# Attention by chunks and a two-layer network: the second layer's C11 seeded in PSUM, three more quarters by seven products, other fillers, and a fixed order

## The chip, the cores and the metric

The kernel runs on one core of one Trainium2 chip. The metric is the time of one execution in device microseconds. Seven names are used for the parts of the core: PE is TensorE (matmuls), PEld its weight loads, DVE VectorE, ACT ScalarE, POOL GpSimd, SP SyncE (it issues DMAs), and PSUM is the memory that TensorE writes, in 8 banks of 2 KB for each of 128 partitions.

## What is computed

```python
# q, k, v: 8 x 8 heads x 576 x 64;  w_in: 512 x 2048;  w_out: 2048 x 512
scores = (q_c @ k_c^T) / 8            # in chunks of 64 tokens
attn   = exp(scores - max) / (sum + 1e-9)
x      = (attn @ v_c)                 # 4608 tokens x 512
h      = x @ w_in
g      = max(0.01 * h, h)
out    = g @ w_out                    # 4608 x 512, float32
```

## The kernel before

**Units of attention.** The 4608 tokens are cut into 36 units of 128 tokens (two chunks, all heads). For a unit u GpSimd issues the loads of q and k (line 93), with a cast to fp16. For the first ten units TensorE transposes q and k (pe_t, lines 404 and 409) against an identity that GpSimd makes; later SyncE does it by DMA (lines 428 and 431). q is put, zero-padded, into QZ (lines 118, 120, 444), and k into KT. The scores go to PSUM (s, tile Sp, line 451). VectorE takes the maximum (m, line 461), subtracts it (b, line 465), ScalarE exponentiates (x, line 471), VectorE sums (z, line 477), adds 1e-9 (ze, line 479), takes the reciprocal (zi, line 481), and VectorE or GpSimd normalises (n, line 487). The result is transposed (e on TensorE, line 495, and its copy d2; or d by DMA, line 506), multiplied with v (v, tile xp, line 517), and ScalarE casts the product into xT (a, line 530), the transposed input of the network, a ring of 1536 tokens. v lies in VB with zeros beside it; for the first batch it is loaded in rows (v_t, line 127) and put in place by copies (v_p).

**Blocks of the network.** The tokens form 12 blocks: 0 to 3 of 128 tokens, 4 to 11 of 512. The plain first layer, mm1(j, a, h), multiplies a column block a of w_in with tokens (tile hT, line 185); for a block of 128 tokens a column block has 512 columns and 16 matmuls. w_in arrives in eight loads, two for each column block of 512 (Q0 to Q3, line 135), w_out in four (P0 to P3, line 141). ScalarE applies the leaky function into gT (line 196). The plain second layer, mm2, serves blocks 0 to 3 (tile oP, line 210).

**Seven products.** For the other blocks matrices are cut in two by two, and the four quarters of a result are made from seven products instead of eight, with sums of the inputs formed ahead: VF and WF of the weights (lines 232 and 235), XF of the tokens (x_form, line 283), S0, S1 and two in-place sums of gT (g_form, lines 342 to 350). Products 1, 6, 7 and 4 pass one after another through a running sum in bank A, products 5 and 3 through bank C, and product 2 uses bank B; C11 is p1 + p2:

```python
B: p2 (with p1: C11)
A: p1, then p6 on top (a copy u2 is taken), p7 (copy u3), p4 (C21)
C: p5 (plus u3 gives C22), p3 on top (plus u2 gives C12)
```

In the first layer (first_fast, tiles hA, hB, hC, line 323) a quarter of a block's columns at a time is treated so; FAST says how many of a block's four quarters, the rest being plain: 4, 3, 4, 2, 4, 4 for blocks 6 to 11, 21 in all. UNIT = 256 cuts blocks 6 and 7 into two halves of 256 tokens each, so that a product there has matmuls of 128 columns in place of 256. In this layer ScalarE seeds bank B with p1 (the step d), and p2 adds to it there. In the second layer (second_fast, tiles oA, oB, oC, line 371), products of blocks 4 to 11 are halved, p = 0 and 1, eight matmuls of 256 columns each. There the step d copies p1 to a temporary, p2 opens its own bank, and VectorE adds the two into the output tile osb (line 235). For the last block (11) the steps work on halves, so that stores can start early.

**What sets the order.** Every step is a Step with its engine, an assumed duration, its inputs, a key, and the PSUM banks and temporaries that it takes and gives. A planner, run(), keeps a clock for each engine and for two DMA queues, picks the step that can begin first (among those within 0.03 us by its key, with hand-set corrections in TUNE), gives out banks and temporaries, and writes the instructions in that order. An engine carries out its instructions in the order written. A table ON names the engine for steps that have a choice. Where TensorE would wait in the first 40 us, the planner puts fillers there, matmuls of 128 columns on the identity (idle, line 535).

Of the kernel before, what the change touches and what calls it, by code (L numbers as in the profile page):

```python
# [16 lines left out]
def kernel(  # L17
# [15 lines left out]
    CH = 64  # L33
# [19 lines left out]
    FAST = {6: 4, 7: 3, 8: 4, 9: 2, 10: 4, 11: 4}  # L53
    UNIT = {6: 256, 7: 256}
    POOL_N, POOL_X, POOL_S = 9, 20, 20
# [139 lines left out]
    def leaky(to, of):  # L195
        nc.scalar.activation(out=to, in_=of, func=AFT.Prelu, bias=0.0, scale=1.0, alpha=0.01)  # L196

    def copy(to, of):
        nc.scalar.activation(out=to, in_=of, func=AFT.Copy, bias=0.0, scale=1.0)  # L199
# [23 lines left out]
    def evict2(j, ti):  # L223
        OSB[j, ti] = osb_tile()[:, 0]
        copy(OSB[j, ti], OP.pop((j, ti)))
# [52 lines left out]
    def x_form(j, h, i):  # L278
# [3 lines left out]
        def less(to, a, b):  # L282
            (nc.gpsimd if j >= POOL_X else nc.vector).tensor_tensor(out=to, in0=a, in1=b, op=ALU.subtract)
# [53 lines left out]
    def g_form(j, i):  # L337
# [5 lines left out]
        if i == 0:  # L343
            plus(SF[j, 0], a21, a22)
        elif i == 1:
            minus(SF[j, 1], SF[j, 0], a11)
        elif i == 2:
            (nc.gpsimd if j >= POOL_S else nc.vector).tensor_tensor(out=a21, in0=a11, in1=a21, op=ALU.subtract)
        else:
            (nc.gpsimd if j >= POOL_S else nc.vector).tensor_tensor(out=a12, in0=a12, in1=SF[j, 1], op=ALU.subtract)  # L350

    def out_product(j, m, p, tag=None):
# [6 lines left out]
        }[m]  # L359
        if j == LAST:  # L360
            key = (j, p, "o" + IN[m])
            if m in OPENS:
                PA[key] = bank([128, HM], "o" + IN[m], tag)
            to, fresh = PA[key], m in OPENS
        else:
            key = (j, "o" + IN[m])
            if m in OPENS and p == 0:
                PA[key] = bank([128, 2, HM], "o" + IN[m], tag)
            to, fresh = PA[key][:, p, :], m in OPENS and p == 0
# [46 lines left out]
    def stage_k(u):  # L416
        KT[u] = sbp.tile([128, 4, 2, CH], FP16, name="KT", tag="KT", bufs=4)
        nc.scalar.activation(out=KT[u], in_=KP.pop(u), func=AFT.Copy, bias=0.0, scale=1.0)
# [50 lines left out]
    def stage_x(u):  # L469
        E[u] = sbp.tile([128, 8, CH], FP16, name="ex", tag="ex", bufs=2)  # L470
        nc.scalar.activation(out=E[u], in_=SH.pop(u), func=AFT.Exp, bias=0.0, scale=SCL)  # L471

    ZI: dict[int, bass.AP] = {}

    def stage_z(u):
        z = sbp.tile([128, 8], FP32, name="z", tag="z", bufs=2)
        nc.vector.tensor_reduce(out=z, in_=E[u], axis=AXL.X, op=ALU.add)  # L477
        ze = sbp.tile([128, 8], FP32, name="ze", tag="ze", bufs=2)
        nc.vector.tensor_scalar_add(out=ze, in0=z, scalar1=1e-9)
        ZI[u] = sbp.tile([128, 8], FP32, name="zi", tag="zi", bufs=2)  # L480
        nc.vector.reciprocal(out=ZI[u], in_=ze)  # L481
# [45 lines left out]
    def stage_a(u):  # L527
        xp = XP.pop(u)
        at = u * G % RING
        nc.scalar.activation(out=xT[:, :, at:at + G], in_=xp, func=AFT.Copy, bias=0.0, scale=1.0)  # L530

    def idle(n, tag):
        t = bank([128, 4, 128], "idle", tag)
        for i in range(n):
            nc.tensor.matmul(out=t[:, i % 4, :], lhsT=ident, rhs=ident, start=True, stop=True)  # L535
# [21 lines left out]
    class Hold:  # L557
# [3 lines left out]
        def fits(self, slots):  # L561
            return [y for y in slots if not self.written or y[1] in written]

    written: set = set()

    class Step:
# [12 lines left out]
    free: dict[str, list[tuple[float, object]]] = {  # L579
        "bank": [(0.0, x) for x in BANKS], "tmp": [(0.0, x) for x in range(NTMP)],  # L580
    }

    class Queues:

        def __init__(self):
            self.now, self.ring, self.out, self.n = 0.0, ([], []), ({}, {}), [0, 0]
            self.done, self.still = 0, []  # L590

        def matmuls(self, n, t):
            self.done += n
            if self.done >= 140:
                self.done -= 128
                if t > STALLS_FROM:
                    self.still.append((t + 0.75, t + 0.75 + STALL))

        def put(self, q, step, at, packets, slow):
            self.ring[q].append([at, packets, slow, step])  # L600
            self.n[q] += 1

        def heads(self):
            return [r[0] if r and r[0][0] <= self.now + 1e-9 else None for r in self.ring]

        def rates(self, h):
            if any(a - 1e-9 <= self.now < b - 1e-9 for a, b in self.still):
                return (0.0, 0.0)
            if h[0] and h[1]:
                return (370.0, 695.0 / h[1][2]) if h[1][2] > 1 else (425.0, 399.0)  # L610
            return (ALONE[0] if h[0] else 0.0, ALONE[1] / h[1][2] if h[1] else 0.0)

        def event(self):
            h = self.heads()
            v = self.rates(h)
            t = [self.now + x[1] / y for x, y in zip(h, v) if x and y]
            t += [r[0][0] for r, x in zip(self.ring, h) if r and not x]
            if any(h):
# [615 lines left out]
```

## Time and profile before

| | |
|---|---|
| time, median of 3 runs | 275.9 us (275.85 to 277.14) |
| profiled execution: span | 273.8 us (from its first to its last instruction; the profile gives no other time of this execution) |
| matmuls / weight loads | 3406 / 3406, of them 86 fillers, all before 18.35 us |
| granted clock of TensorE | 1.00 in every slice |
| DMA | 38.27 MB in 162004 packets; GpSimd's queue carried 18.09 MB, SyncE's 19.41 MB |
| first product of the first layer | 18.35 us |
| end of the last matmul | 270.43 us |

The page of the profile gives busy time by engine, by line and by slice; its views answer for a stretch, a line or a tile. "Idle before" is the time for which an engine stood still ahead of an instruction, and behind it stands what ended the wait. In a view by windows the columns after the stretch and its length are the busy times of PE, PEld, DVE, ACT and POOL with the number of instructions, then the granted clock, the DMA share and GB/s. In a timeline the first two columns are start and length in us. Ends of matmuls are modelled, so a group of matmuls is measured from its start to the next one's start.

### The profile page before, as it was taken

The page shows a single profiled execution, that of the slowest core. Times are in us where ns is not written, and L with a number is a line of the kernel's source. Part 1 is how long each engine was busy: PE and PEld are TensorE (multiplying, and loading weights), DVE is VectorE, ACT ScalarE, POOL GpSimd, SP SyncE. Part 2 cuts the span into 40 slices and gives each one's busy share as a digit, 9 for nine tenths or more (in the row PEclk, how much of TensorE's full clock was granted, in tenths as well). Part 3 has the DMA queues.
Part 4 walks back from the last instruction along what each step waited for, and adds up shares of the span by engine and source line. Part 5 has one row for each costly group of instructions (what it writes and reads, how often), then busy time and mean ns, then how long its engine had stood idle before and what let it go on. Part 6 is the DMA issues. An engine that isn't in the chain of part 4 may idle for free.

```text
span 273.8 us, 8229 instructions
## 1 busy us (share of the span) xinstructions
PE 263.2 (96%) x3406; PEld 238.2 (87%) x3406; DVE 208.2 (76%) x375; ACT 193.9 (71%) x359; POOL 158.9 (58%) x198
## 2 busy tenths in 40 slices
PE   1999999999999999999999999999999999999995
PEld 1889578799999999999999999899999989888884
DVE  5895285789978898899788999897879865831671
ACT  6588947778475644999796369978866896378721
POOL 8999783967898959587758778657351000000000
PEclk9999999999999999999999999999999999999999
DMA  9999999999999999999999999999954100220233
GB/s 134 154 191 183 182 176 176 155 173 217 151 158 152 120 143 208 170 144 234 154 155 121 136 140 247 133 186 197 136 84 151 43 19 2 77 79 0 79 115 116
DMA packets 162004, 38.27 MB, mean 140 GB/s; under 512 B 153008, under 2 KB 157616, under 8 KB 161968
## 3 DMA queue, kind: packets, MB, share of 16 engines
q0 software_dynamic: 114384, 18.09, 97.0%
q1 hardware_dynamic: 46544, 19.41, 42.2%
q8 instruction: 26, 0.43, 0.6%
q10 hardware_dynamic: 1040, 0.26, 0.4%
q14 instruction: 10, 0.08, 0.2%
HBM read 36.70 MB, written 9.44 MB: 169 GB/s over the span
## 4 chain that ended last, share of the span: by engine, by line
PE 90%; ACT 3%; DMA 3%; POOL 2%; issue 1%; DVE 0%; POOLq 0%
PE oA L371 20%; PE hT L185 17%; PE hA L323 14%; PE oC L371 10%; PE hC L323 7%; PE oP L210 5%; PE oB L371 5%; PE hB L323 3%; PE Sp L451 3%; PE xp L517 3%; DMA q_in<-in_q_dram 3%; PE tpe L495 1%; PE idle L535 1%; ACT gT L196 1%; ACT xT L530 1%; PE qp L404 1%
## 5 line engine op out<-in xcount | busy, mean ns | idle before, releaser
L371 PEld LDWEIGHTS <-gT 128*128 128x128 f16 x640 | 61.1, 98 | 6.6
L185 PE MATMUL hT<-xT,w_inT 128*128 128x128 f16 (+1 forms) x864 | 58.6, 225 | 0.1
L185 PEld LDWEIGHTS <-w_inT 128*128 128x128 f16 x864 | 53.1, 98 | 2.0 <-issue 0.4
L444 POOL COPY QZ<-QT 64x512 f16<-64x512 f16 x52 | 36.6, 705 | 20.0 <-DMA QT<-q_in 13.1
L196 ACT ACTIVATE gT<-hT 128x512 f16<-128x512 f32 x60 | 35.1, 599 | 15.9 <-PE hT L185 15.6
L235 DVE TENSOR_TENSOR tmp<-hC,tmp 128x512 f32<-128x512 f32 x42 | 27.9, 678 | 16.6 <-PE hC L323 8.3
L487 POOL TENSOR_TENSOR en<-ex,zi 128x512 f16<-128x512 f16 x22 | 23.8, 1083 | 26.8 <-DVE zi L481 12.3
L323 PEld LDWEIGHTS <-VF 128*128 128x128 f16 x448 | 34.5, 98 | 2.4
L93 POOL DMA_DIRECT2D q_in<-in_q_dram x39 | 33.8, 871 | 4.5 <-DMA w_outT<-in_moe_w_out_dram 1.8
L93 POOL DMA_DIRECT2D k_in<-in_k_dram x39 | 33.5, 863 | 1.2 <-DMA VB<-in_v_dram 0.8
L461 DVE TENSOR_REDUCE mx<-Sp 128x8 f32<-128x512 f32 x36 | 24.6, 684 | 10.3 <-PE Sp L451 10.2
L371 PE MATMUL oA<-WF,gT 128*128 128x256 f16 x256 | 32.2, 273 | 0.0
L199 ACT ACTIVATE tmp<-hA 128x512 f32<-128x512 f32 x42 | 24.3, 602 | 6.8 <-PE hA L323 6.8
L196 ACT ACTIVATE gT<-tmp 128x512 f16<-128x512 f32 x42 | 26.4, 634 | 3.7 <-DVE tmp L235 3.6
L323 PEld LDWEIGHTS <-w_inT 128*128 128x128 f16 x336 | 26.2, 98 | 1.9
L471 ACT ACTIVATE ex<-sh 128x512 f16<-128x512 f32 x36 | 22.8, 633 | 7.0 <-DVE sh L465 6.8
L371 PEld LDWEIGHTS <-S 128*128 128x128 f16 x256 | 24.6, 98 | 2.8
L477 DVE TENSOR_REDUCE z<-ex 128x8 f32<-128x512 f16 x36 | 24.3, 676 | 3.3 <-ACT ex L471 3.2
L530 ACT ACTIVATE xT<-xp 128x512 f16<-128x512 f32 x36 | 21.4, 597 | 7.6 <-PE xp L517 7.4
L465 DVE TENSOR_TENSOR sh<-Sp,mx 128x512 f32<-128x512 f32 x36 | 24.5, 681 | 0.6
L323 PE MATMUL hA<-XF,VF 128*128 128x128 f16 (+1 forms) x224 | 24.7, 246 | 0.0
L199 ACT ACTIVATE tmp<-oA 128x512 f32<-128x512 f32 (+1 forms) x27 | 14.9, 552 | 11.7 <-PE oA L371 11.6
(76 smaller groups left out, 478.7 us busy)
## 6 DMA issues: line engine op xcount, KB each, us to landing
out_dram<-osb SPq DMA_DIRECT2D x14, 512.0 KB, 5.2
VB<-in_v_dram POOLq DMA_DIRECT2D x14, 288.0 KB, 9.1
q_in<-in_q_dram POOLq DMA_DIRECT2D x31, 128.0 KB, 8.3
k_in<-in_k_dram POOLq DMA_DIRECT2D x31, 128.0 KB, 8.4
w_inT<-in_moe_w_in_dram POOLq DMA_DIRECT2D x8, 256.0 KB, 7.5
w_outT<-in_moe_w_out_dram POOLq DMA_DIRECT2D x4, 512.0 KB, 9.0
out_dram<-osb SPq DMA_DIRECT2D x6, 256.0 KB, 5.5
v_t<-in_v_dram POOLq DMA_DIRECT2D x4, 128.0 KB, 7.0
```

Source lines behind the costliest of these rows:

```text
L93: nc.gpsimd.dma_start(out=t[a - u * G:z - u * G], in_=src[b, :, r:r + z - a, :].rearrange("h p d -> p h d"))
L185: nc.tensor.matmul(out=hT[:, i, :], lhsT=w_inT[:, t, fc * 128:(fc + 1) * 128], rhs=xT[:, t, r0 % RING:r0 % RING + tb], start=(i == 0 and t ...
L196: nc.scalar.activation(out=to, in_=of, func=AFT.Prelu, bias=0.0, scale=1.0, alpha=0.01)
L199: nc.scalar.activation(out=to, in_=of, func=AFT.Copy, bias=0.0, scale=1.0)
L235: (nc.vector if e == "dve" else nc.gpsimd).tensor_tensor(out=to, in0=a, in1=b, op=ALU.add)
L323: nc.tensor.matmul(out=PA[key][:, c, :], lhsT=w[:, t, fc * 128:(fc + 1) * 128], rhs=x[:, t, :], start=(m in (1, 5) and c == 0 and t == 0), ...
L371: nc.tensor.matmul(out=to, lhsT=lhs[:, fc, p * 128:(p + 1) * 128], rhs=rhs[:, fc, :], start=(fresh and fc == 0), stop=(fc == HB - 1), skip ...
L444: nc.gpsimd.tensor_copy(out=QZ[u % NQZ][part, :, :, s, :], in_=QT[u][part].rearrange("p i (e t) -> p i e t", e=2))
L461: nc.vector.tensor_reduce(out=MX[u], in_=SP[u], axis=AXL.X, op=ALU.max)
L465: nc.vector.tensor_tensor(out=SH[u], in0=SP.pop(u), in1=MX.pop(u).unsqueeze(2).to_broadcast((128, 8, CH)), op=ALU.subtract)
L477: nc.vector.tensor_reduce(out=z, in_=E[u], axis=AXL.X, op=ALU.add)
L530: nc.scalar.activation(out=xT[:, :, at:at + G], in_=xp, func=AFT.Copy, bias=0.0, scale=1.0)
```

## The change

Six things change.

1. In the second layer the step d copies p1 from bank A into bank B (on ScalarE; in the last block on VectorE), product 2 adds to it there, and a new step c11 copies bank B to osb. VectorE's sum for C11 and the temporary for it go. Product 2 now has the seed among its inputs.
2. FAST is 4 for blocks 7 and 9 too: 24 quarters by seven products instead of 21. No plain quarter is left in blocks 6 to 11.
3. The fillers are matmuls of up to 512 columns on a tile of ones, which VectorE sets with its first instruction (in the memory of XF); the identity isn't needed for them.
4. The three steps of the softmax's denominator become separate (z, ze, zi), and ze may run on ScalarE.
5. More steps have a choice of engine: k, a, copies, seeds, the leaky function (as a two-operand instruction on VectorE), sums for the products (on GpSimd).
6. The planner goes. In its place stand a table ORDER (1478 rows: the number of a step, its fillers, its banks) and a full table ON.

```diff
-    FAST = {6: 4, 7: 3, 8: 4, 9: 2, 10: 4, 11: 4}
+    FAST = {6: 4, 7: 4, 8: 4, 9: 4, 10: 4, 11: 4}
...
+    ones = XF[0][:, 0].rearrange("p t n -> p (t n)")
+    nc.vector.memset(ones, 1.0)
...
-    def leaky(to, of):
-        nc.scalar.activation(out=to, in_=of, func=AFT.Prelu, bias=0.0, scale=1.0, alpha=0.01)
+    def leaky(to, of, e="act"):
+        if e == "act":
+            nc.scalar.activation(out=to, in_=of, func=AFT.Prelu, bias=0.0, scale=1.0, alpha=0.01)
+        else:
+            nc.vector.scalar_tensor_tensor(out=to, in0=of, scalar=0.01, in1=of, op0=ALU.mult, op1=ALU.max)
...
     def idle(n, tag):
-        t = bank([128, 4, 128], "idle", tag)
-        for i in range(n):
-            nc.tensor.matmul(out=t[:, i % 4, :], lhsT=ident, rhs=ident, start=True, stop=True)
+        t = bank([128, 512], "idle", tag)
+        while n:
+            w = min(n, 4) * 128
+            nc.tensor.matmul(out=t[:, :w], lhsT=ones[:, :128], rhs=ones[:, :w], start=True, stop=True)
+            n -= w // 128
...
     def out_product(j, m, p, tag=None):
...
+        opens = m in OPENS and m != 2
...
     def run():
...
+        for i, fill, *slots in ORDER:
+            s = steps[i]
+            if fill:
+                idle(fill[0], BANKS[fill[1]])
+            for h, slot in zip(s.take, slots):
+                h.slot = BANKS[slot] if h.pool == "bank" else slot
             s.emit()
...
+    ORDER = [
+        (57, 0), (6, 0), (56, 0), (8, 0), (66, 0), (60, 0), (55, 0), (1, 0), (63, 0), (65, 0), (58, 0), (0, 0), (62, 0), (2, 0), (53, 0), (13, 0), (52, 0), (61, 0),
...
     def second_fast(j, k0):
...
-        d = cp("d", p1)
-        p2 = mm(2, [g(1, 0) + [p1[1]]] * 2)
+        d = []
+        for p in ps:
+            e, t = on(key + ("d", p), "act", act=us[0], dve=us[1])
+            def seed(p=p, e=e):
+                at = (j, p, "oB") if last else (j, "oB")
+                PA[at] = bank([128, HM] if last else [128, 2, HM], "oB", B1[p].slot)
+                copy(PA[at], psum("oA", p), e)
+            d.append(add(key + ("d", p), e, t, seed, [p1[p]] if last else p1, key=7.0 + k0 / 100, take=[B1[p]]))
+        p2 = mm(2, [[y, p1[1]] + g(1, 0) for y in (d if last else d * 2)])
...
-        s11 = sum_of("d", 0, lo, [x + osb_free() for x in two(p2, d)], B1)
+        s11 = []
+        for p in ps:
+            e, t = on(key + ("c11", p), "act", act=us[0], dve=us[1])
+            s11.append(add(key + ("c11", p), e, t, lambda p=p, e=e: copy(dest(0, lo, p), psum("oB", p), e), ([p2[p]] if last else p2) + osb_free(), key=1.5 + k0 / 100, give=[B1[p]]))
```

Three places show how instructions move. The first is GpSimd's queue at the very start (loads and the identity). The loads of q_in, k_in and v_t are those of units 1 to 3 and of v's first rows; each w_inT row is half of a column block. Before:

```order
L93 DMA q_in<-in_q_dram 128x8x64
L93 DMA k_in<-in_k_dram 128x8x64 x2
L135 DMA w_inT<-in_moe_w_in_dram 64x4x512 x2
masks.py:197 MEMSET ident 128x128
masks.py:199 ISA
masks.py:199 AFFINE_SELECT ident<-ident 128x128
L93 DMA q_in<-in_q_dram 128x8x64 x2
L127 DMA v_t<-in_v_dram 128x8x64 x3
```

And now:

```order
L95 DMA q_in<-in_q_dram 128x8x64
L129 DMA v_t<-in_v_dram 128x8x64
L95 DMA k_in<-in_k_dram 128x8x64
L95 DMA q_in<-in_q_dram 128x8x64
L95 DMA k_in<-in_k_dram 128x8x64
L129 DMA v_t<-in_v_dram 128x8x64
L95 DMA q_in<-in_q_dram 128x8x64
masks.py:197 MEMSET ident 128x128
masks.py:199 ISA
masks.py:199 AFFINE_SELECT ident<-ident 128x128
L137 DMA w_inT<-in_moe_w_in_dram 64x4x512
L95 DMA k_in<-in_k_dram 128x8x64
```

The identity stands behind seven loads instead of five, and the first w_in behind it. Through the last load of the third column block both orders have the same fifteen loads: six of q and k, three of v, six of w_in.

The second place is TensorE at the first products of the first layer, with the semaphores that an instruction waits for (DMASW: a load from GpSimd's queue; rows of the same group left out). Before:

```order
L185 LDWEIGHTS w_inT [waits DMASW4_49,DMASW3_49]
L185 MATMUL hT<-xT,w_inT 128x128 [waits Activation_49]
...
L451 LDWEIGHTS QZ [waits DVE_49]
...
L185 LDWEIGHTS w_inT [waits DMASW4_49,DMASW3_49]
...
L495 LDWEIGHTS en [waits DVE_49]
...
L185 LDWEIGHTS w_inT [waits DMASW6_49,DMASW5_49]
```

And now:

```order
L189 LDWEIGHTS w_inT [waits DMASW2_49,DMASW1_49]
L189 MATMUL hT<-xT,w_inT 128x128 [waits DVE_49]
...
L543 LDWEIGHTS VB_63 [waits Activation_49]
...
L189 LDWEIGHTS w_inT [waits DMASW7_49,DMASW3_49]
...
L459 LDWEIGHTS QZ [waits Activation_49]
...
L189 LDWEIGHTS w_inT [waits DMASW6_49,DMASW5_49]
```

The three rows with two DMASW are the first uses of the column blocks 0, 1 and 2 of w_in. Before, two groups (blocks 0 and 1) came from column block 0 and two from column block 1 ahead of the third column block, and between them a unit's scores, transposed attention and product with v; now there is one group from each. The first group waits for VectorE, which now casts the first xT, where it was ScalarE.

The third place is VectorE at the last block's second layer (S are S0 and S1 of gT). Before:

```order
L235 TENSOR_TENSOR osb<-oB,tmp 128x256
L235 TENSOR_TENSOR S_5180<-gT 128x2048
L235 TENSOR_TENSOR osb<-oB,tmp 128x256
L232 TENSOR_TENSOR S_5191<-S_5180,gT 128x2048
L348 TENSOR_TENSOR gT<-gT 128x8x256
L350 TENSOR_TENSOR gT<-gT,S_5191 128x8x256
L235 TENSOR_TENSOR osb<-oC,tmp 128x256 x4
```

And now:

```order
L242 TENSOR_TENSOR S_5116<-gT 128x2048
L122 COPY oB<-oA 128x256
L239 TENSOR_TENSOR S_5136<-S_5116,gT 128x2048
L242 TENSOR_TENSOR osb<-oC,tmp 128x2x256
L122 COPY oB<-oA 128x256
L122 COPY osb<-oA 128x2x256
L239 TENSOR_TENSOR gT<-gT 128x8x256
L122 COPY osb<-oB 128x256
```

The two sums of oB and a temporary have gone; two seeds (oB<-oA) and copies stand there, and the last sum of gT, a12 - S1, is GpSimd's last instruction now. On TensorE the last product was number 3 (oC) and is now number 4 (oA).

More of the change, by code (lines that the diff above doesn't have):

```diff
@@ L1027, in act @@
         def act(name, f, e, after):
[L1028 removed]
+            by, us = on(key + ("g" + name,), "act", act=0.52, dve=0.61)
+            made_of(f, e, add(key + ("g" + name,), by, us, lambda: leaky(g_part(j, h, i, f, e), TMP[key + (name,)], by), after + gone(j), key=8.0 + k0, give=[T[name]]))
         xs = x_of(j, h * w, (h + 1) * w)
```

337 lines of the change are left out of this document (109 added, 228 removed), and 162 rows, old and new, of tables (ON, ORDER).

## The prediction

> **What bounds the kernel now.** The page's first lines come first: TensorE is busy nearly throughout, the others have room on average. Then the view of the waits, for TensorE alone, and busy time by stages.
>
> ```profile
> PE 263.2 (96%) x3406; PEld 238.2 (87%) x3406; DVE 208.2 (76%) x375; ACT 193.9 (71%) x359; POOL 158.9 (58%) x198
> PE kp L409 <- POOL ident masks.py:199: 6.0, 1, 6.0
> PE qp L404 <- DMA q_in<-in_q_dram: 0.4, 1, 0.4
> 18.35:42.00 23.65, 23.27 (x319) 18.14 (x316) 13.96 (x31) 18.52 (x33) 20.93 (x28) 1.00 1.79 181
> 42.00:260.00 218.00, 217.93 (x2838) 200.23 (x2836) 174.17 (x305) 160.32 (x297) 121.34 (x144) 1.00 1.42 136
> 260.00:270.45 10.45, 10.41 (x96) 9.08 (x93) 5.85 (x8) 2.90 (x7) 0.00 (x0) 1.00 0.31 114
> 270.45:273.80 3.35, 0.00 (x0) 0.00 (x0) 0.42 (x1) 0.00 (x0) 0.00 (x0) 1.00 0.33 118
> ```
>
> In the rows by stage, length comes first, then TensorE's busy time. From 42 us to 270.45 it misses 0.1 us. So there the time is the sum of its instructions; nothing on another engine can help unless it removes matmuls, and anything that makes TensorE wait costs in full. That leaves three places: matmul work, the start (until 42 us), and the 3.35 us behind the last matmul. The span is 273.8 us and the median of the runs 275.9, so 2.1 us lie around the span; I carry them over.
>
> **Fewer products.** Here are pieces of the chain that ended last, then of the timeline (start, length).
>
> ```profile
> 129.56 2.62 PE hT L185 x24
> 158.06 0.87 PE hA L323 x8
> 138.04 0.61 PE L323 MATMUL hC<-XF,VF 128*128 128x128 f16 x8
> 138.49 0.61 PE L323 MATMUL hC<-xT,VF 128*128 128x128 f16 x8
> ```
>
> A plain quarter is four groups of eight matmuls of 256 columns, 2.62/3 = 0.873 each: 3.49 us. By seven products of four such matmuls it is 7 x 0.87/2 = 3.05. In block 7 a product is eight matmuls of 128 columns, 138.49 - 138.04 = 0.45 us, and the quarter 3.13. Two quarters of block 9 save 0.44 each, one of block 7 saves 0.36: **-1.24 us**. Their sums of tokens exist already, since both blocks had fast quarters. The new work on other engines is 3 x (3 copies or activations, 2 sums); below.
>
> **C11 in PSUM.** It takes no matmul away.
>
> ```profile
> L235 DVE TENSOR_TENSOR osb<-oB,tmp 128x512 f32<-128x512 f32 x7 | 4.8, 687 | 2.0 <-PE oB L371 1.1 <-ACT tmp L199 0.9
> L199 ACT ACTIVATE hB<-hA 128x512 f32<-128x512 f32 x21 | 12.0, 588 | 8.0 <-PE hA L323 7.7
> L479 DVE TENSOR_SCALAR ze<-z 128x8 f32<-128x8 f32 x36 | 10.2, 282 | 1.2
> L232 DVE TENSOR_TENSOR WF<-w_outT,WF 128x2048 f16<-128x2048 f16 x2 | 2.4, 1195 | 0.0
> ```
>
> Per block a sum of 0.69 us leaves VectorE and a copy out of PSUM arrives, 0.6. What is new is the wait: product 2 now stands behind the seed (0.59, as the first layer's), and with it all of TensorE's queue. In the new order at least 1.35 us of other products lie between product 1's end and product 2 (block 6; in the others 1.55 to 7.5), so with some 0.3 us of hand-over at both ends the seed is covered: 0. Without that cover a block would lose 0.6 to 0.9 us. The small sums of the softmax go largely to ScalarE (27 x 0.28 off VectorE), nine casts of xT, 13 leaky activations and some 25 copies come to VectorE. Counting every moved instruction by such rows, VectorE gains some 13 us, ScalarE loses 12, GpSimd gains 26; VectorE's 208 become some 221 of 274. Nothing is gained by that while TensorE has no wait; what it may cost is between 0 and the second rival's price. I take 0, nearest to the 0.1 us that TensorE misses now with VectorE at 80% in that stage.
>
> **The start.** Landing times of loads issued by GpSimd decide here. The rows show GpSimd's issues, then issues by their window with the time from issue to landing, then TensorE.
>
> ```profile
> 1.25 1.06 POOL L93 DMA_DIRECT2D q_in<-in_q_dram  x1 [0.80 <-POOLq L1218]
> 2.31 1.76 POOL L93 DMA_DIRECT2D k_in<-in_k_dram  x2
> 5.62 0.29 POOL masks.py:199 TENSOR_SCALAR_AFFINE_SELECT ident<-ident 128x128 f16<-128x128 f16 x1
> 14.16 0.61 POOL L135 DMA_DIRECT2D w_inT<-in_moe_w_in_dram  x1 [0.19 <-issue]
> w_inT<-in_moe_w_in_dram POOLq DMA_DIRECT2D x1, 256.0 KB, 8.2
> 18.35 2.17 PE L185 MATMUL hT<-xT,w_inT 128*128 128x128 f16 x32
> 23.06 2.84 PE L185 MATMUL hT<-xT,w_inT 128*128 128x128 f16 x48
> 8.08 0.63 PE L451 MATMUL Sp<-KT,QZ 128*128 128x64 f16 x8
> ```
>
> The third column block of w_in is complete with the fifteenth load: 14.16 + 8.2 = 22.36 us. Its first use is at 23.06 us, so the start runs 0.7 us behind the loads. In the new order the same fifteen loads come first in another sequence, so 22.4 us is the upper estimate of that landing. The lower: the first k_in lands at 7.2 and the second w_in at 12.3 (issue plus latency); a k_in and two w_in took 5.1 us there against 3.35 at the later pace (0.85 and 1.25). If that loss came from w_in standing at the head, it goes: 20.6.
>
> ```profile
> 8.76 0.69 DVE L461 TENSOR_REDUCE mx<-Sp 128x8 f32<-128x512 f32 x1 [0.28 <-PE Sp L451]
> 9.48 0.69 DVE L465 TENSOR_TENSOR sh<-Sp,mx 128x512 f32<-128x512 f32 x1
> 10.09 0.68 DVE L461 TENSOR_REDUCE mx<-Sp 128x8 f32<-128x512 f32 x1
> 7.01 0.86 DVE L120 COPY QZ<-qp 64x512 f16<-64x512 f16 x2 [1.32 <-PE qp L404]
> ```
>
> But TensorE can be late by itself. The identity now follows seven loads of 0.88 us instead of five: it is ready at 8.2 instead of 5.9. Transposes (0.45), one QZ and two KT copies on VectorE (0.43, 0.35, 0.35) put the first scores at 9.5 instead of 8.08 and their maximum at 9.95. From there VectorE runs, start to start, three maxima, two sums z (0.71 each, 9.48 - 8.76 and the like), three subtractions and two normalisations (0.61 each), three more copies (1.2), two reciprocals (0.24 each), and then the cast of xT, 0.69, which ScalarE did before: 9.0 us and some 0.3 of waits for ScalarE, so the first xT stands at 19.2 and the first product of the first layer at 19.3, against 18.35. Two groups (0.89 each), xp and scores (0.24 each) later the third column block is reached at 21.6. So it starts at 21.6 to 22.4. Before, four groups were through by 23.06; now the fourth ends 2.25 us behind that start (two groups, a transpose, an xp): 23.85 to 24.65. TensorE is 0.8 to 1.6 us late there, and wins back up to the 0.38 us that it misses between 18.35 and 42. I take **+0.4**, the end that the pace of the later w_in loads and VectorE's own chain give; the bounds are -0.3 (VectorE's chain 0.7 shorter and loads early) and +1.6. The fillers in themselves cost nothing: the old ones, too, only fill time before the first product.
>
> **The end.**
>
> ```profile
> 270.45 0.42 DVE L235 TENSOR_TENSOR osb<-oC,tmp 128x256 f32<-128x256 f32 x1 [1.32 <-PE oC L371]
> out_dram<-osb SPq DMA_DIRECT2D x1, 256.0 KB, 2.0
> out_dram<-osb SPq DMA_DIRECT2D x1, 128.0 KB, 1.7
> ```
>
> The last matmul was product 3, followed by a sum (0.42) and a store of 128 KB (1.7). Now it is product 4, a copy on ScalarE (0.38) and a store of 256 KB (2.0): **+0.3**.
>
> **Sum**: -1.24 + 0.4 + 0.3 + 0 = -0.54; span 273.3, time **275.4 us**. A measurement of this kernel tells a change from none beyond about 0.5%, 1.4 us; so this is "the same", chance 0.55, with 274.5 to 277.0 as its own range.
>
> **Rivals.**
>
> First, the start gets better: loads at the early end, and fillers that begin at 1.4 us, as the memset of ones needs no identity, so that the first transposes and scores run on a warm clock.
>
> ```profile
> 6.34 1.06 PE L404 MATMUL qp<-ident,q_in 128*128 128x128 f16 x8
> 9.66 3.11 PE L535 MATMUL idle<-ident 128*128 128x128 f16 x40
> 15.75 1.23 PE L535 MATMUL idle<-ident 128*128 128x128 f16 x19
> ```
>
> Eight early matmuls take 7.25 - 6.34 = 0.91 us, 0.114 each; nineteen late ones 1.23, 0.065 each. If each of the four early steps on the path to the scores gains 0.2 us, VectorE's chain 0.7, and the loads allow it, TensorE comes out 0.5 us earlier than now: -1.24 - 0.5 + 0.3 = -1.44, 274.4 us. Against it speak the identity's 2.3 us delay and the cast on VectorE. Faster: 0.27.
>
> Second, slower: GpSimd's 128x2048 sum in the last block. There product 3 waits for a12 - S1, which can begin when product 2 is through; six groups, 5.24 us, lie between, 4.9 after hand-overs. VectorE did it in 1.2 us. GpSimd shows no such operation.
>
> ```profile
> L487 POOL TENSOR_TENSOR en<-ex,zi 128x512 f16<-128x512 f16 x22 | 23.8, 1083 | 26.8 <-DVE zi L481 12.3 <-ACT gT L196 9.1 <-ACT tmp L199 3.3
> 54.54 1.84 POOL L487 TENSOR_TENSOR en<-ex,zi 128x512 f16<-128x512 f16 x1 [0.39 <-DVE zi L481]
> ```
>
> Four times 1.08 are 4.3 us and just fit; below, nothing is won by it. Four times the one of 1.84, 7.4 us, come 2.5 us late: 277.9. It decides from 4.9 us on, and the run is slower by 0.5% from about 6.8. The same price stands for a VectorE that is held up at the three other such sums. The Trainium skill ("SBUF — State Buffer", Who interferes with whom) has a VectorE instruction with two SBUF inputs and a GpSimd instruction that reads SBUF block each other in full, whichever comes first. The one long normalisation of 1.84 us agrees; by that rule the f2 sum ahead of it on VectorE (1.24) delays GpSimd's start by up to 0.4 us, which leaves 4.5, still enough at 4.3. Slower: 0.13.
>
> Third, the clock falls back. 10.5 fillers of 512 columns at 0.107 per 128 last 4.5 us, from 1.4 to 5.9; until the identity, 8.2, TensorE then stands still for 2.3 us. If it went back to the slow pace, the 7.9 us of fillers and transposes up to the first product would take up to twice as long: at most +4.5, near 280. The longest pause that the trace shows after the warm-up is 0.35 us, so it can't exclude this. The Trainium skill ("TensorE: Matmul & The Clock Gate", Part 1) has the clock halved by default and again after an idle window of about 3.4 us. By that 2.3 us are too short on most starts, and the sum stays. Slower: 0.05.
>
> Chances: same 0.55, faster 0.27, slower 0.18. The range 273.7 to 277.8 takes in the first rival, the start's bounds and most of the second; the third stays out, and a start better still.
>
> **What would show it.** Right: TensorE without a wait from about 45 us on, with the first product at about 19.3 us, the third column block at about 22, seeds (oB<-oA) without a TensorE wait behind them, and the last matmul about 0.8 us earlier than 270.4. Wrong in the start: first product before 18.4, or after 20.5. Wrong in the middle: rows "PE oB <- ACT" or "PE hA <- DVE" above 0.5 us, or TensorE's oC behind GpSimd's gT near the end. Wrong in size: hT of 256 columns gone and the work between 42 us and the end not 1.2 us less.

## The result, and the profile after

The changed kernel takes **290.3 us** (median of 4 runs, 289.5 to 292.2) beside 276.5 us of the kernel before: ratio 1.047, 95% interval 1.042 to 1.052. It is slower by 13.8 us, and the forecast was 275.4 us. Here and below the ratios count fast runs alone, so they differ a little from those of the medians (1.050 here). The profiled execution has a span of 290.4 us, before 273.8.

First the page of the kernel after: busy time of the engines, the granted clock in 40 slices, the chain that ended last. The last line is the chain of the kernel before.

```profile
PE 271.0 (93%) x3371; PEld 236.9 (82%) x3371; DVE 237.2 (82%) x383; ACT 178.4 (61%) x355; POOL 186.9 (64%) x210
...
PEclk9799999997999999999999999999999999879999
...
PE 78%; DVE 14%; POOL 2%; ACT 2%; issue 2%; DVEq 0%; POOLq 0%
...
PE 90%; ACT 3%; DMA 3%; POOL 2%; issue 1%; DVE 0%; POOLq 0%
```

VectorE had 0% of the chain before, now 14%, and the clock drops in three places: at the start, at 66 us, at 255 us. TensorE's view of the waits (in total, times, longest) names who is waited for:

```profile
PE tpe L521 <- DVE en L513: 3.6, 2, 3.3
PE oA L379 <- DVE S L239: 3.5, 1, 3.5
PE hC L330 <- DVE tmp L242: 2.3, 2, 1.5
PE qp L412 <- POOL ident masks.py:199: 2.2, 1, 2.2
...
PE oB L379 <- DVE oB L122: 0.5, 1, 0.5
```

9.4 us of waits stand behind three VectorE tiles. None of the rows names a seed on ScalarE; the one wait on a seed (last row) is in block 5, whose seed, like the last block's, VectorE makes. None names one of the five sums of 128x2048 that the change gives to GpSimd. What VectorE did there shows in the timelines of VectorE and of GpSimd (start, length, engine, line, operation):

```profile
60.09 6.76 DVE L513 TENSOR_TENSOR en<-ex,zi 128x512 f16<-128x512 f16 x1
...
152.19 2.28 DVE L239 TENSOR_TENSOR XF<-xT,XF 128x256 f16<-128x256 f16 x1
...
247.75 5.10 DVE L239 TENSOR_TENSOR S<-S,gT 128x2048 f16<-128x2048 f16 x1
```

```profile
59.70 1.15 POOL L113 DMA_DIRECT2D VB<-in_v_dram  x1
60.84 1.38 POOL L95 DMA_DIRECT2D k_in<-in_k_dram  x2
62.20 4.09 POOL L242 TENSOR_TENSOR VF<-w_inT 128x2048 f16<-128x2048 f16 x1
...
247.73 4.05 POOL L239 TENSOR_TENSOR gT<-gT 128x2048 f16<-128x2048 f16 x1 [2.36 <-DVE S L242]
```

A normalisation that took 0.69 us takes 6.76, and a sum S1 of 1.2 us takes 5.10. Both end about 0.5 to 1 us behind one of the five sums. The waits on tmp have two causes: 0.75 us stand behind a normalisation that another of the five held up (3.27 us at 231.12), and 1.5 us behind the sum of x in the middle row, 2.28 us long, which ends just behind a GpSimd normalisation of 128x512. In groups (busy time, mean ns of one) the same two kinds were 687 and 1218 ns before (first two rows: before; last two: after):

```profile
L232 DVE TENSOR_TENSOR S<-S,gT 128x2048 f16<-128x2048 f16 x8 | 9.7, 1218 | 0.1
...
L487 DVE TENSOR_TENSOR en<-ex,zi 128x512 f16<-128x512 f16 x14 | 9.6, 687 | 0.1
...
L513 DVE TENSOR_TENSOR en<-ex,zi 128x512 f16<-128x512 f16 x17 | 23.8, 1399 | 0.2
...
L239 DVE TENSOR_TENSOR S<-S,gT 128x2048 f16<-128x2048 f16 x8 | 13.9, 1736 | 0.2
```

Last the view by windows around the two long pauses: stretch, length, busy times of PE, PEld, DVE, ACT, POOL, then TensorE's clock.

```profile
63.50:66.90 3.40, 0.08 (x1) 0.00 (x0) 3.40 (x3) 0.00 (x0) 2.79 (x1) 1.00 1.74 207
66.90:70.80 3.90, 3.89 (x37) 3.45 (x38) 3.41 (x6) 1.51 (x3) 3.32 (x4) 0.56 0.42 108
...
249.40:252.90 3.50, 0.05 (x1) 0.00 (x0) 3.50 (x2) 0.73 (x2) 2.38 (x1) 0.81 0.00 0
252.90:258.41 5.51, 5.50 (x26) 3.90 (x27) 2.01 (x4) 0.60 (x1) 0.00 (x0) 0.50 0.51 190
```

TensorE stands still for 3.3 us and for 3.5 us, and behind each pause it runs 3.9 us at 0.56 and 5.5 us at 0.50 of its clock, which loses 1.7 and 2.7 us more. These two places together: 3.33 + 3.47 + 1.7 + 2.7 = 11.2 of the 13.8 us.

### The profile page after: what moved, and what is told of

It is laid out like the page before. It is cut to its first block, busy times and chain, and to the rows that moved or that the text cites. A ratio compares the mean times of both kernels' runs of the same rounds, so it can differ in the third digit from the quotient of the medians.

```text
span 290.4 us, 8217 instructions
## 1 busy us (share of the span) xinstructions
PE 271.0 (93%) x3371; PEld 236.9 (82%) x3371; DVE 237.2 (82%) x383; ACT 178.4 (61%) x355; POOL 186.9 (64%) x210
## 4 chain that ended last, share of the span: by engine, by line
PE 78%; DVE 14%; POOL 2%; ACT 2%; issue 2%; DVEq 0%; POOLq 0%
PE oA L379 17%; PE hT L189 13%; PE hA L330 13%; PE oC L379 9%; PE hC L330 7%; DVE en L513 5%; PE oB L379 4%; PE oP L217 3%; PE hB L330 3%; PE Sp L459 3%; PE xp L543 3%; DVE S L239 2%; DVE tmp L242 1%; PE qp L412 1%; ACT QZ L120 1%
## 5 line engine op out<-in xcount | busy, mean ns | idle before, releaser
L189 PE MATMUL hT<-xT,w_inT 128*128 128x128 f16 x768 | 48.3, 221 | 0.6 <-issue 0.4
L189 PEld LDWEIGHTS <-w_inT 128*128 128x128 f16 x768 | 45.0, 99 | 1.9 <-issue 0.9
L330 PEld LDWEIGHTS <-VF 128*128 128x128 f16 x512 | 40.6, 99 | 6.0 <-issue 2.6
L242 DVE TENSOR_TENSOR tmp<-hC,tmp 128x512 f32<-128x512 f32 x48 | 32.2, 682 | 8.4 <-PE hC L330 6.7
L513 POOL TENSOR_TENSOR en<-ex,zi 128x512 f16<-128x512 f16 x19 | 21.2, 1119 | 27.8 <-DVE zi L505 17.2
L201 ACT ACTIVATE gT<-hT 128x512 f16<-128x512 f32 x48 | 27.0, 597 | 10.6 <-PE hT L189 10.3
L330 PEld LDWEIGHTS <-w_inT 128*128 128x128 f16 x384 | 30.1, 98 | 2.2
L239 POOL TENSOR_TENSOR gT<-gT,S 128x2048 f16<-128x2048 f16 x3 | 12.2, 4058 | 28.6 <-DVE tmp L122 26.9
L330 PE MATMUL hA<-XF,VF 128*128 128x128 f16 (+1 forms) x256 | 28.1, 248 | 0.0
L513 DVE TENSOR_TENSOR en<-ex,zi 128x512 f16<-128x512 f16 x17 | 23.8, 1399 | 0.2
L201 ACT ACTIVATE gT<-tmp 128x512 f16<-128x512 f32 x35 | 21.3, 628 | 1.8 <-DVE tmp L242 1.8
```

Of the source, the lines that this page charges most:

```text
L189: nc.tensor.matmul(out=hT[:, i, :], lhsT=w_inT[:, t, fc * 128:(fc + 1) * 128], rhs=xT[:, t, r0 % RING:r0 % RING + tb], start=(i == 0 and t ...
L242: (nc.vector if e == "dve" else nc.gpsimd).tensor_tensor(out=to, in0=a, in1=b, op=ALU.add)
L330: nc.tensor.matmul(out=PA[key][:, c, :], lhsT=w[:, t, fc * 128:(fc + 1) * 128], rhs=x[:, t, :], start=(m in (1, 5) and c == 0 and t == 0), ...
L513: eng.tensor_tensor(out=E[u], in0=ex, in1=ZI.pop(u).unsqueeze(2).to_broadcast((128, 8, CH)), op=ALU.mult)
```

## The experiments

The theory: a GpSimd sum that reads SBUF holds up VectorE instructions that read two SBUF tiles, TensorE runs out of work behind them, and its clock falls. Its rivals: VectorE has simply too much to do; the start is what costs; a sum is late by itself, being more than three times as long on GpSimd. The table of waits already speaks against the last one in the changed kernel, since TensorE waits for none of the five sums there.

**1. The five large sums back on VectorE** (order and all else kept; the entries of the table ON are put together in one line here).

```diff
-('vf', 0): 'pool', ('sf', 4, 3): 'pool', ('sf', 9, 3): 'pool', ('sf', 10, 2): 'pool', ('sf', 11, 3): 'pool'
+('vf', 0): 'dve',  ('sf', 4, 3): 'dve',  ('sf', 9, 3): 'dve',  ('sf', 10, 2): 'dve',  ('sf', 11, 3): 'dve'
```

> The changed kernel with its five sums of 128x2048 (first of the four weight sums of layer one; fourth sum of the second layer in blocks 4, 9 and 11, third in block 10) moved from GpSimd back to VectorE, order and everything else kept. Held-up theory (a GpSimd sum keeps VectorE's two-input instructions waiting for its whole length, TensorE pauses behind them and its clock halves): the pauses at 63.5 and 249 us and the half clock behind them go, no 128x512 multiply of VectorE takes over 1.5 us, time 277 to 282 (9 to 13 us back of the 13.8 that separate it from the kernel before). Rival, VectorE simply has too much to do: five sums of some 1.3 us more on it, so 288 to 296. Rival, the start and its cold clock are the main loss: 287 to 290.

Measured: 279.1 us, ratio to before 1.007 (1.004 to 1.010). So 4.0 of the 4.7% come back, 11.0 us of 277.5. By the medians, each beside the kernel before of its own series, it is 12.3 of the 13.8 us. The page and the groups of this run:

```profile
PE 266.5 (96%) x3371; PEld 234.4 (84%) x3371; DVE 225.6 (81%) x388; ACT 178.5 (64%) x355; POOL 163.7 (59%) x205
...
L513 DVE TENSOR_TENSOR en<-ex,zi 128x512 f16<-128x512 f16 x17 | 12.5, 738 | 0.2
```

VectorE has five sums more (6.2 us) and is busy 11.6 us less: so about 17.8 us of its "busy" time was waiting. A view of busy time does not tell the two apart; a group's mean against its mean in another run does. The rival of an overloaded VectorE falls here.

**2. Only the two sums beside the long pauses** (the first weight sum; the third sum of block 10).

```diff
-('vf', 0): 'pool', ('sf', 10, 2): 'pool'
+('vf', 0): 'dve',  ('sf', 10, 2): 'dve'
```

> Only the two sums whose held-up VectorE instructions end in a pause of over 3 us of TensorE are moved back to VectorE (first weight sum of layer one, third sum of the second layer in block 10); the three others stay on GpSimd. Held-up theory: most of the gain of the run with all five, time 279 to 284, and in blocks 4 and 9 a VectorE multiply of about 3.2 us is still there with TensorE waits of 0.5 to 0.8 us. Rival, overloaded VectorE: no gain, 288 to 293. Rival, start: 287 to 290.

Measured: 280.0 us, ratio 1.0075 (1.004 to 1.011), as with all five. The sums left on GpSimd still hold VectorE, as its row and GpSimd's (the next fence) show:

```profile
225.69 3.27 DVE L513 TENSOR_TENSOR en<-ex,zi 128x512 f16<-128x512 f16 x1
```

```profile
224.35 4.06 POOL L239 TENSOR_TENSOR gT<-gT,S 128x2048 f16<-128x2048 f16 x1
```

but TensorE's longest wait for VectorE is 0.7 us. So the price of a held-up instruction is set by who waits for it: two of five cost nearly everything.

**3. The eleven sums of x on VectorE as well.**

```diff
-('xf', 6, 0, 2): 'pool', ('xf', 6, 1, 0): 'pool', ... ('xf', 11, 0, 2): 'pool'
+('xf', 6, 0, 2): 'dve',  ('xf', 6, 1, 0): 'dve',  ... ('xf', 11, 0, 2): 'dve'
```

> As the run with five sums on VectorE, and the eleven sums of x (128x256 and 128x512 elements) that GpSimd has go to VectorE too. Held-up theory: these hold VectorE for at most about 1 us each and little of that reaches TensorE, so within 1.5 us of the run with five sums, likelier below. Rival, overloaded VectorE: 2 to 5 us longer than the run with five sums.

Measured: 278.8 us, ratio 1.005 (1.0015 to 1.009); repeated later with more runs (the tenth experiment below) 279.1 us, 1.007 (1.0035 to 1.0105). That is the run with five sums, within the error: as the theory had it.

**4. The kernel before, with four of these sums issued on GpSimd**, in its own order.

```diff
-(nc.gpsimd if j >= POOL_S else nc.vector).tensor_tensor(out=a21, ...
+(nc.gpsimd if j == 10 else nc.vector).tensor_tensor(out=a21, ...
-(nc.gpsimd if j >= POOL_S else nc.vector).tensor_tensor(out=a12, ...
+(nc.gpsimd if j in (4, 9) else nc.vector).tensor_tensor(out=a12, ...
-in_form(q_, e)
+in_form(q_, "dve" if q_ else "pool")
```

> The kernel before with four of its 128x2048 sums issued on GpSimd in place of VectorE (first weight sum of layer one, fourth sum of the second layer in blocks 4 and 9, third in block 10), its order kept. Held-up theory: VectorE instructions of 2 to 6 us appear beside the four sums and TensorE waits behind them, 279 to 286. Rival, GpSimd's sums cost nothing and VectorE gains 5 us of free time: 274 to 277. A late sum alone (4.1 us in place of 1.2, with nothing held up) would make products that read it wait up to 2.9 us each: 276 to 285, but with VectorE's instructions at their usual lengths.

Measured: 287.5 us, ratio 1.033 (1.025 to 1.042), slower than any of the forecasts. A loss of that kind appears in the other kernel too, but TensorE's largest waits come another way. VectorE, GpSimd and TensorE at the first sum:

```profile
70.43 3.81 DVE L479 TENSOR_SCALAR ze<-z 128x8 f32<-128x8 f32 x1
74.34 0.20 DVE L481 RECIPROCAL zi<-ze 128x8 f32<-128x8 f32 x1
```

```profile
69.93 4.07 POOL L235 TENSOR_TENSOR VF<-w_inT 128x2048 f16<-128x2048 f16 x1
73.94 0.92 POOL L93 DMA_DIRECT2D q_in<-in_q_dram  x1
74.87 1.45 POOL L487 TENSOR_TENSOR en<-ex,zi 128x512 f16<-128x512 f16 x1
```

```profile
76.38 0.40 PE L495 MATMUL tpe<-ident,en 128*128 128x128 f16 x4 [4.26 <-POOL en L487]
```

Even an addition of 1e-9 to eight numbers a partition waits for the sum's end (3.81 us; 0.17 is usual), and the reciprocal behind it is ready at 74.54. But the normalisation that TensorE waits for, by 4.26 us, is GpSimd's own here: it stands behind the sum and a load issue in GpSimd's queue until 74.87, so it would have begun as late with nothing held up on VectorE. In the same way TensorE waits 2.3 us for a copy to QZ that stood behind another of the sums. So this run shows the hold-up again, but the price of its two largest waits is that of GpSimd's own queue.

**5. Who holds up whom**, measured by itself, one section for each kind of VectorE instruction (cut short):

```diff
+P.tensor_tensor(out=sums, in0=big, in1=big2, op=ALU.add)      # 128x2048, or copies, a fill, load issues
+for i in range(3):
+    KINDS[kind](i)                                            # VectorE, 128x512, started beside it
```

> The kernel's own work is left out; in its place 29 short sections, each with three VectorE instructions of one kind on 128x512 elements, first with GpSimd idle (ten kinds), then started 0.5 us or more after a GpSimd sum of 128x2048 began (the same ten), then beside GpSimd copies of 128x1024, a GpSimd fill of 128x2048 and GpSimd issues of loads (three kinds each). Held-up theory: beside the sum the kinds with two inputs in SBUF (sum of two f16 tiles, multiply by a broadcast, sum of two f32 tiles, leaky step) show a first instruction of 2 to 4 us that ends with the sum, and the other two at the length they have alone; the kinds with one SBUF input or one in PSUM keep within 20% of their length alone. Rival, a mere slowdown (shared bandwidth): all three instructions of a section are longer by the same share, none over 1.5 us. Rival, no effect of GpSimd at all: every kind within 10% of its length alone.

The timeline of VectorE, three instructions a row, first with GpSimd idle, then beside its sum:

```profile
10.85 1.90 DVE L55 TENSOR_TENSOR to<-half,z 128x512 f16<-128x512 f16 x3 [0.62 <-ACT z L85]
...
15.48 1.89 DVE L57 SCALAR_TENSOR_TENSOR to<-full 128x512 f16<-128x512 f32 x3 [0.32 <-ACT full L85]
19.50 1.87 DVE L59 CAST to<-acc 128x512 f16<-128x512 f32 x3
...
22.36 1.87 DVE L61 TENSOR_REDUCE to<-half 128x8 f32<-128x512 f16 x3 [0.38 <-ACT half L85]
...
31.86 8.94 DVE L55 TENSOR_TENSOR to<-half,z 128x512 f16<-128x512 f16 x3 [0.57 <-ACT z L85]
...
47.34 5.75 DVE L57 SCALAR_TENSOR_TENSOR to<-full 128x512 f16<-128x512 f32 x3 [0.32 <-ACT full L85]
55.21 1.88 DVE L59 CAST to<-acc 128x512 f16<-128x512 f32 x3
...
59.06 4.56 DVE L60 COPY to<-half 128x512 f16<-128x512 f16 x3 [1.98 <-ACT half L85]
63.95 1.87 DVE L61 TENSOR_REDUCE to<-half 128x8 f32<-128x512 f16 x3 [0.32 <-ACT half L85]
```

With two inputs in SBUF, three multiplies go from 1.90 to 8.94 us (the first is held by one sum, the third by the next, and the second runs between them) and three leaky steps from 1.89 to 5.75. A cast out of PSUM (tile acc) and a reduction do not change, 1.88 and 1.87. Of three sums with one input in PSUM only the last ran beside a GpSimd sum; it kept its 0.68 us. The forecast had plain f16 copies unaffected; they are held too (0.68 to 4.56), and so is the small addition (0.32 to 3.94). Beside load issues the multiplies keep 1.90, while the copies take 1.65. The rival of a mere slowdown falls, and so does "no effect".

**6. The start in another order**, all sums on VectorE: the identity behind three loads, and ScalarE's conversion of k first.

```diff
-(1, 0), (63, 0), ... (7, 0), (5, 0), (12, 0), (24, 0), (54, 0),
+(1, 0), (5, 0), (63, 0), ... (7, 0), (54, 0), (12, 0), (24, 0),
```

> The changed kernel with all its sums on VectorE, and the start alone reordered: the identity on GpSimd is made behind three loads in place of seven, and ScalarE converts its half of the first k ahead of placing V rows. Start theory (the identity and that conversion, at 8.3 and 7.9 us, make the first product 1.7 us late): first product at 18.0 to 18.9 us, time 1.3 to 2.2 us below the run with all sums on VectorE, 276.5 to 277.5. Rival, the loads set the start (each load behind the identity comes 0.6 us later): first product no earlier than 19.9, time within 0.5 us of that run.

Measured: 279.6 us, ratio 1.0105 (1.001 to 1.020): no gain. The wait for the identity is gone, but in the profiled execution, the longest of four, the first product comes later, not earlier. TensorE's timeline, then VectorE's:

```profile
7.99 0.61 PE L417 MATMUL kp<-ident,k_in 128*128 128x128 f16 x4 [1.37 <-DMA k_in<-in_k_dram]
...
22.56 1.05 PE L189 MATMUL hT<-xT,w_inT 128*128 128x128 f16 x16 [0.20 <-DMA q_in<-in_q_dram]
```

```profile
11.55 0.43 DVE L122 COPY QZ<-qp 64x512 f16<-64x512 f16 x1 [1.77 <-ACT QZ L120]
12.01 0.69 DVE L473 TENSOR_TENSOR sh<-Sp,mx 128x512 f32<-128x512 f32 x1
```

The loads moved back, and VectorE's queue makes the first unit wait for the second: its subtraction stands behind a copy that waits for the q of the second unit.

**7 and 11. C11 summed by VectorE again**, all sums on VectorE. Product 2 opens its own bank again, the plain copy goes to the output tile, and VectorE adds the bank to it (the main lines of the edit).

```diff
-copy(PA[at], psum("oA", p), e)                     # the seed
+copy(dest(0, lo, p), psum("oA", p), e)
-copy(dest(0, lo, p), psum("oB", p), e)
+plus(dest(0, lo, p), psum("oB", p), dest(0, lo, p))
```

> The changed kernel with all its sums on VectorE, and C11 alone taken back: product 2 opens its own bank, the copy of product 1 goes to the output tile in SBUF and VectorE adds the bank to it, in place of the seed in PSUM and a plain copy. Theory that the seed is covered and its sum was never on the path: within 0.7 us of the run with all sums on VectorE. Rival, the seed delays product 2: 1 us or more shorter. Rival, VectorE is the bound and the seed relieves it: 1.5 to 4 us longer.

> C11 summed by VectorE in place of the seed, all else as in the run with all sums on VectorE, once more beside it on one chip. Theory that the seed is covered: within 0.7 us of that run. Rival, the seed costs: 1 us or more shorter. Rival, it relieves VectorE: 1 us or more longer.

Measured: 281.3 us, ratio 1.018 (1.005 to 1.030); again, beside its counterpart on one chip, 280.8 us, 1.012 (1.007 to 1.017), against 279.1 us and 1.007 (1.0035 to 1.0105) with the seed. The seed does not cost; in this order, which was laid out for it, it is likelier worth about 1.6 us. The forecast of at most 0.7 us between the two was missed by the medians (1.6 and more), in the direction of a seed that relieves VectorE. But the intervals overlap, so the size stays open. The trace of the first of the two has one wait that fits, 1.0 us of TensorE for a subtraction of VectorE.

**8. The kernel before with 24 quarters by seven products**, laid out by its planner without a search.

```diff
-FAST = {6: 4, 7: 3, 8: 4, 9: 2, 10: 4, 11: 4}
+FAST = {6: 4, 7: 4, 8: 4, 9: 4, 10: 4, 11: 4}
```

> The kernel before, its own planner, with 24 instead of 21 quarters by seven products and nothing else of the change; the planner lays the order out anew, with no search. The matrix work falls by 1.24 us (3 quarters of 0.41). Forecast by that term alone: 275 to 277.5 beside a kernel before of 276 to 278, so 0 to 1.3 us shorter. Rival, three more quarters (each with four copies, two sums and four leaky steps) load VectorE and ScalarE so that TensorE waits: 278 to 283.

Measured: 280.5 us, ratio 1.014 (1.003 to 1.025), where the term alone had 275 to 277.5. The view of the waits has new ones of 1.7, 0.9 and 0.7 us for VectorE and ScalarE, in the first layer and at xT, where the kernel before had none above 0.4 us behind the identity; a load at the start makes TensorE wait 1.8 us besides. Three quarters' saving, 1.24 us, is worth less than what comes with them as long as the order does not hide that.

**9 and 10. More fillers**, all sums on VectorE, beside the same without them.

```diff
-(83, (42, 0), 0)
+(83, (80, 0), 0)
```

> The changed kernel with all its sums on VectorE, and the first fillers alone made longer: 80 instead of 42 columns blocks, so that TensorE works until about the identity (8.3 us) instead of stopping at 6.0. Theory that the half clock from 8.3 to 13 us is what the start loses beside the identity: the transposes at 8.3 take 0.22 to 0.25 us in place of 0.38 to 0.61, the first product comes 0.8 to 1.5 us earlier, time 0.5 to 1.5 us below the run with all sums on VectorE of the same call. Rival, the chain of VectorE, ScalarE and loads sets the first product whatever TensorE's clock: within 0.4 us of that run. Rival, the clock falls back anyway in the pauses between the transposes: first product within 0.4 us, and the fillers at 11.5 us still at half clock.

> The run with all sums on VectorE once more, to stand beside the two others of this call on one chip: 0.5% above the kernel before, as the first time (interval 0.15 to 0.9%).

Measured: 279.5 us, 1.009 (1.005 to 1.012), against 279.1 us, 1.007 (1.0035 to 1.0105). The clock is full to the end, and the first product is no earlier (20.09 us without the fillers):

```profile
20.58 1.05 PE L189 MATMUL hT<-xT,w_inT 128*128 128x128 f16 x16 [0.20 <-DVE xT L122]
```

So the cold clock at the start costs nothing that can be measured here. That leaves loads, VectorE and ScalarE to set the first product.

**12. A queued sum, and pauses**, measured by themselves: load issues with and without a sum behind them, and runs of 60 matmuls with pauses (cut short).

```diff
+for t in qs:
+    P.dma_start(out=t, in_=...)                   # two issues
+if behind:
+    P.tensor_tensor(out=sums, in0=big, in1=big2, op=ALU.add)
+for n in (1, 2, 3, 4, 5, 6, 8):
+    60 matmuls of 512 columns, then n copies on ScalarE that the next matmul waits for
```

> The kernel's own work is left out; two things are measured by themselves. First, three VectorE instructions with two SBUF inputs started with two load issues on GpSimd, once with nothing behind these and once with a sum of 128x2048 queued right behind. If the sum holds VectorE only while it runs itself, the three run at their usual 0.4 to 0.65 us each before it begins; if it holds VectorE from when it is queued (what the 6.8 us multiply beside two issues and a sum would say), one of them takes over 5 us. Second, runs of 60 matmuls of 512 columns (0.22 us each at full clock) with pauses of about 0.9 to 5 us between them, made by one to eight copies on ScalarE. Theory that a pause of some 3 us halves the clock for about 4 us: after the pauses up to 2 us the 60 matmuls take 13 us, after those from 3 us on about 15 us, the first at 0.44 us each. Rival, the pause does not matter and the half clock had another cause: 13 us after every pause.

VectorE's rows: three multiplies beside issues alone; then two of the three f16 sums and the first multiply with a GpSimd sum queued behind the issues. Below them the two GpSimd sums; the last issue began at 13.16 in the one case and at 25.67 in the other:

```profile
20.49 1.90 DVE L65 TENSOR_TENSOR to<-half,z 128x512 f16<-128x512 f16 x3 [1.69 <-ACT z L51]
...
13.18 0.43 DVE L67 TENSOR_TENSOR to<-half,half 128x512 f16<-128x512 f16 x1 [3.95 <-ACT half L51]
13.53 4.95 DVE L67 TENSOR_TENSOR to<-half,half 128x512 f16<-128x512 f16 x1
...
25.79 5.38 DVE L65 TENSOR_TENSOR to<-half,z 128x512 f16<-128x512 f16 x1 [3.40 <-ACT z L51]
```

```profile
14.12 4.06 POOL L62 TENSOR_TENSOR sums<-big,big 128x2048 f16<-128x2048 f16 x1
...
26.55 4.06 POOL L62 TENSOR_TENSOR sums<-big,big 128x2048 f16<-128x2048 f16 x1
```

With nothing behind the issues the three multiplies are through in 1.90 us. With the sum queued the first of them begins 0.76 us ahead of it, more time than the 0.69 that one needs, and still ends 0.56 us behind the sum's end: it was held while the sum waited behind an issue. Of the f16 sums the first, begun together with that issue, still ran at its 0.43 us; the second was held from 0.59 us ahead. The normalisation of 6.76 us in the changed kernel is of this kind, though its 2.1 us ahead of the sum, past more than one issue, were not measured by themselves. TensorE's runs of 60 (in brackets the pause ahead):

```profile
94.02 14.80 PE L75 MATMUL acc<-half,w 128*128 128x512 f16 x60 [2.63 <-ACT to L51]
...
130.48 13.11 PE L75 MATMUL acc<-half,w 128*128 128x512 f16 x60 [3.89 <-ACT to L51]
```

Pauses of 0.7, 1.4 and 2.0 us cost only themselves; 2.6, 3.3 and 5.1 us cost 1.4 to 1.8 us more; 3.9 us did not, against the forecast. The record of the granted clock shows why. In this trace its half-clock stretches last 3.41 us or twice that, and begin and end on points 3.41 us apart. In the view by windows, cut at these points (TensorE's busy time is the first number behind the length):

```profile
91.05:94.46 3.41, 0.78 (x5) 0.26 (x4) 0.00 (x0) 2.39 (x4) 0.00 (x0) 1.00 0.01 2
...
125.18:128.59 3.41, 1.41 (x7) 0.54 (x6) 0.00 (x0) 1.81 (x4) 0.00 (x0) 1.00 0.00 0
...
142.25:145.66 3.41, 1.34 (x7) 0.49 (x5) 0.00 (x0) 1.88 (x4) 0.00 (x0) 1.00 0.00 0
```

The pause of 2.6 us lies in one such stretch and leaves 0.78 us of work in it, and the next stretch runs at half clock. The one of 3.9 us falls into two, with 1.41 and 1.52 us of work, and the clock stays. The first part of the one of 5.1 us leaves 1.34 us, and the clock falls. In the changed kernel the stretches before the two falls have 0.35 and 1.28 us of work. So what counted in these traces was the work in such a stretch, with the limit between 1.35 us (experiment 4) and 1.41 us of 3.41, and a pause of about 3 us is a risk, not a certainty: it depends on where it falls.

## Why the prediction was wrong, step by step

- **The moved work, taken at 0: the step that failed.** The prediction counted 13 us more on VectorE and 26 us more on GpSimd and took 0, as TensorE had no wait before. It measured 11 to 12.5 us (experiments 1 to 3). Busy time was the wrong measure: VectorE had room for the five sums (experiment 1), but not for standing still while GpSimd made them.
- **The second rival had the mechanism, at the wrong place and price.** It looked at the sum of the last block, and there it was right: 4.05 us of GpSimd fit ahead of product 3. It gave "the same price", at most 2.5 us, to the three other such sums and overlooked a fourth, the weight sum VF, and it never asked which VectorE instruction runs beside each sum and who waits for it. At VF and in block 10 it was one that TensorE needed next: 3.3 and 3.5 us of pause, with 1.7 and 2.7 us lost to half clock behind them. The Trainium skill ("SBUF — State Buffer", Who interferes with whom) has an instruction of VectorE with two SBUF inputs and a reading one of GpSimd block each other in full, and likewise a copy in a two-port mode; experiment 5 agrees with both (1.90 to 8.94 us; 0.68 to 4.56). The rule stood in the prediction and was worked out at one place of five.
- **The third rival**, a clock that falls back, was put at the start with up to 4.5 us. There the clock did fall (0.87 from 10 to 20 us), at no cost (experiment 9). It cost 4.4 us where the prediction had expected no pause, and a pause of 2.6 us was enough for it in experiment 12, so 3.4 us of idle time are not needed.
- **The start, taken at +0.4, bounds -0.3 to +1.6: too small.** With all sums on VectorE the last matmul of the tenth experiment ends at 272.3 us, 1.9 later than before; adding the 1.24 us of saved products and taking off 1.3 us of waits behind 42 us leaves 1.8 us at the start, in the third experiment's trace 2.6. Moving the identity and warming the clock each brought no gain (experiments 6 and 9). These sizes come from single traces, in which waits for loads at the start differ (0.6 us in the tenth experiment's, 1.8 in the ninth's). The first product came at 20.05 us, not 19.3, and the third column block at 22.5, just behind the forecast's 21.6 to 22.4. Loads and VectorE's order of queue stay as its likely cause; what would cure it is open.
- **The quarters, -1.24 us: not seen alone.** Where they were the only change (experiment 8), waits of 3.3 us on VectorE and ScalarE came with them.
- **C11, taken at 0: right or better.** In the changed kernel's second layer no TensorE wait stands behind a seed of ScalarE, and without the seed the kernel is no faster (experiments 7 and 11).
- **The end, +0.3:** from the end of the last matmul to the end of the span it is 4.1 us instead of 3.35, so 0.7.

Together: by the ratios 11 to 11.5 of 13.0 us belong to the sums, by the medians 12.3 to 12.6 of 13.8. What is left is 2.6 us between the spans of the tenth experiment (276.4) and of before (273.8): 1.8 for the start, 0.7 for the end, 1.3 for waits behind 42 us (1.2 of them on a transposed k), less 1.2 for the quarters; by medians and ratios it is 1.2 to 1.9. None of the versions that ran beats the kernel before.

## What to carry to other kernels

When work moves to GpSimd, do not ask whether GpSimd has time; for each moved instruction that reads SBUF, look up which VectorE instruction stands beside it in the order, whether that one reads two SBUF tiles, and who waits for it. Price it by the whole GpSimd instruction and by the issues queued ahead of it, and where TensorE then pauses for some 3 us, reckon with 1.4 to 2.7 us more for half clock. Look also at what stands behind the sum in GpSimd's own queue: that waits too (4.3 and 2.3 us of TensorE in experiment 4). Long GpSimd work may go where VectorE has reductions or PSUM operands to do, or nothing that TensorE waits for.

## What was not expected of the hardware

- VectorE was held 0.59 and 0.76 us before the GpSimd sum began, while that stood behind a load issue (experiment 12); in the changed kernel from 60.09 us on, 2.1 us ahead of the sum at 62.20.
- One sum can follow another into the lock: of three multiplies, 8.94 us in all, the third waited for a second sum that began 0.7 us after the first had ended (experiment 5).
- A leaky step that names the same SBUF tile twice counts as two inputs (1.89 to 5.75 us), and an addition on 128x8 is held like a large one (0.32 to 3.94 us for three).
- A pause of 2.6 us halved the clock and one of 3.9 us did not (experiment 12): the clock followed the work in fixed stretches of 3.41 us, and fell behind those with 1.35 us of work or less.
